# Relu-squared attention into an MLP mixer: a straight last step of the first batch, residual transposes issued per step, channel units ahead of the transposes of x, and another order of weight loads

## Chip, cores and metric

One NeuronCore of a Trainium2 chip. The time is device microseconds (us) of one execution. A lower time is better. A run was compared with runs of the kernel before on the same chip, and only fast runs count for the times: some executions of the same kernel run at a lower granted TensorE clock for a while.

Engines are named as the profile names them: PE is TensorE's matrix multiplication, PEld its weight loads, DVE VectorE, ACT ScalarE, POOL GpSimd, SP SyncE (it issues the DMA transposes here).

## The reference

```python
# q, k, v: (8, 12, 448, 64);  d_model = 12*64 = 768;  token width 256;  channel width 1536
scores = (1/sqrt(64)) * q @ k.T
attn   = relu(scores)**2 / 448
x      = (attn @ v)  as (8, 448, 768)                       # heads side by side
u      = x + (relu(x.T @ w_tok1) @ w_tok2).T                # token mixing
out    = u + relu(u @ w_ch1) @ w_ch2                        # channel mixing
```

## The kernel before

Four heads form a **quad**; there are 24, three (DB) per batch item. **Step i** computes the scores of quad i and, for quad i-1, the values (attention times v), the transposes of x, and token mixing (`token1`, `token2`). When the three quads of a batch item are mixed, its channel mixing is put in a queue of **units**: a `channel1` unit is 6 matmuls, 12 units per batch item; `channel2` units are 12 matmuls. `fill` puts units at set places between the other work, to cover PE's waits. From quad 6 on, the transposes of x are DMA transposes issued by SyncE; before that, PE does them. Steps 0 to 3 have a hand-written order; step 3 is the last of the first batch item, and the first step with units to run.

```python
    def values_out(i):                       # scale quad i's values into xT, on DVE
        ...
        for r in range(2):
            nc.vector.tensor_scalar(out=xT[b % 2][:, 2 * d + r, :S], in0=ps[:, r, :S], ...)

    def x_back(i):                           # x with tokens on partitions
        ...
        if i >= XDMA:                        # XDMA = 6: by DMA
            for r in range(2):
                nc.sync.dma_start_transpose(out=x_sb[:, r], in_=xT[b % 2][:, 2 * d + r, :])
            return
        ...                                  # else 8 PE transposes into ps, then
        nc.vector.tensor_copy(...)           # one copy of 1024 columns to x_sb

    def u_back(b):                           # the residual u, tokens on partitions
        t = chunks(b)
        u_tiles[b] = mix.tile([128, NP, NT - NT // 2, 128], BF16, name="u_sb", bufs=3)
        for p in range(NP):                  # NP = 6
            nc.sync.dma_start_transpose(out=u_tiles[b][:, p, : len(t), :],
                                        in_=uT_tiles[b // 2][:, p, t.start * 128 : t.stop * 128])

    def channel_work(b):                     # after token2 of the batch item's last quad
        u_back(b)
        for e in range(EC):                  # EC = 12
            queue.append((C1, lambda e=e: channel1(b, e)))
        ...                                  # channel2 units too

    for i in range(DB + 1):                  # steps 0 to 3
        for c in range(QC):                  # seven chunks of scores
            if i == DB and c < 2:            # step 3
                square()
                values(i - 1, ((4,), (5, 6))[c])
                if c == 1:
                    values_out(i - 1)
            scores(i, c)
            ...
            if i < DB: ...
            else:                            # step 3
                if c == 0: token2(i - 2, early=True)
                if c == 2: x_back(i - 1)
                if c == 3: token1(i - 1)
                if c == 4: transposes(i + 1); token2(i - 1, early=True); channel_work(0)
                if c == 5: fill(1 / 4)
        if i == 1: load_four(4); load_wc1(1, 2)
        if i == 2: load_four(5); load_wc2(0, 4)
        if i == 3: load_four(6); load_wc2(1, 4)
    square()
    fill(1 / 4)

    for i in range(DB + 1, ND + 2):          # steps 4 and on
        ...                                  # scores 0, 1; values(i - 1); values_out(i - 1); scores 2
        x_back(i - 1)
        ...                                  # loads of quad i + 3
        fill(1 / 3)
        ...                                  # scores 3, 4; transposes of q and k of quad i + 1
        fill(2 / 9)
        token1(i - 1)
        fill(1 / 9, least=1)
        ...                                  # scores 5, 6; token2(i - 1); channel_work
        fill(1 / 3)
```

## Time and profile before

| | kernel before |
|---|---|
| time, median of 3 runs | 386.91 us (386.85 to 387.58) |
| span of the profiled run | 385.1 us |
| PE busy | 363.2 us, 94% |
| last-ending chain: PE / DMA | 82% / 10% |

The page's chain of work that ended last, and one of its costliest groups (line, engine, operation, shapes, count; busy us, mean ns of one; idle time just before, and what ended most of it):

```profile
PE 82%; DMA 10%; POOL 3%; DVE 2%; ACT 1%; issue 1%; ACTq 0%
...
L248 PE MATMUL t_ps<-x_sb,wt 128*128 128x256 bf16 x192 | 24.9, 273 | 3.3 <-DMA x_sb<-xT 2.8
```

PE makes most of the chain, but a tenth of it is transfers. The second line is `token1`: of the 3.3 us for which PE stood idle before it in the whole run, 2.8 were for x_sb, which a DMA transpose brings (2.25 of them at one place, near 131 us). The other waits are shown in the prediction.

### The profile page before, as it was taken

How to read it: one execution, taken by the hardware profiler on the slowest of the kernel's cores; microseconds unless marked ns; L12 is line 12 of the kernel's file. 1: busy time of each engine (PE TensorE's matmuls, PEld its weight loads, DVE VectorE, ACT ScalarE, POOL GpSimd, SP SyncE). 2: the span in 40 equal slices, each digit the busy share in tenths (PEclk: the TensorE clock that was granted, in tenths of full speed). 3: DMA queues.
4: the chain of work that ended last, by engine and by line, in shares of the span. 5: the costliest groups of instructions: out<-in, count | busy, mean ns of one | idle time of the engine just before them, and what ended most of it. 6: DMA issues, size and time to landing. Idle time of an engine off the chain costs nothing.

```text
span 385.1 us, 10018 instructions
## 1 busy us (share of the span) xinstructions
PE 363.2 (94%) x4281; PEld 198.9 (52%) x4281; DVE 207.1 (54%) x375; ACT 212.2 (55%) x295; POOL 99.5 (26%) x178
## 2 busy tenths in 40 slices
PE   6778889999999799999999999999999999999995
PEld 2344445544555455555545655555555555555563
DVE  2898657672585565555654756545744755121022
ACT  4987677676465246764676455764576455411400
POOL 9974254503303123303213213123120000000000
PEclk9999999999999999999999999999999999999999
DMA  8999999995549497598449677498453433334024
GB/s 155 130 193 174 179 184 110 188 152 72 78 102 175 102 167 128 63 138 155 97 72 113 122 144 133 61 128 138 115 74 66 92 78 74 64 63 107 2 52 112
DMA packets 72045, 43.82 MB, mean 114 GB/s; under 512 B 46080, under 2 KB 68544, under 8 KB 72000
## 3 DMA queue, kind: packets, MB, share of 16 engines
q0 software_dynamic: 24448, 21.47, 42.0%
q1 hardware_dynamic: 47248, 21.28, 30.5%
q8 instruction: 33, 0.54, 0.6%
q10 hardware_dynamic: 304, 0.43, 0.4%
q14 instruction: 12, 0.10, 0.1%
HBM read 43.38 MB, written 11.01 MB: 141 GB/s over the span
## 4 chain that ended last, share of the span: by engine, by line
PE 82%; DMA 10%; POOL 3%; DVE 2%; ACT 1%; issue 1%; ACTq 0%
PE m_ps L327 28%; PE m_ps L310 27%; PE sc_ps L163 8%; PE acc_ps L191 7%; PE t_ps L248 5%; PE h_ps L272 4%; DMA wc<-in_moe_w_ch_dram 4%; DMA k_raw<-in_k_dram 3%; PE qkT_ps L142 2%; DMA x_sb<-xT 2%; DMA k_first<-in_k_dram 1%; ACT at L172 1%; POOL q_raw L83 1%; DVE xT L205 1%; POOL k_raw L83 1%
## 5 line engine op out<-in xcount | busy, mean ns | idle before, releaser
L172 ACT ACTIVATE at<-sc_ps 128x896 bf16<-128x896 f32 x168 | 144.7, 922 | 60.5 <-PE sc_ps L163 60.5
L310 PE MATMUL m_ps<-uT_sb,wc 128*128 128x448 bf16 x576 | 117.8, 353 | 0.6 <-DVE uT_sb L280 0.6
L327 PE MATMUL m_ps<-wc,r_sb 128*128 128x384 bf16 x672 | 115.3, 326 | 0.0
L179 DVE TENSOR_TENSOR at<-at 128x896 bf16<-128x896 bf16 x168 | 98.5, 626 | 6.1 <-ACT at L172 5.9
L317 ACT ACTIVATE r_sb<-m_ps 128x448 bf16<-128x448 f32 x96 | 52.2, 544 | 65.7 <-PE m_ps L310 65.1
L327 PEld LDWEIGHTS <-r_sb 128*128 128x128 bf16 x672 | 64.3, 98 | 45.7 <-issue 4.1
L310 PEld LDWEIGHTS <-wc 128*128 128x128 bf16 x576 | 54.4, 98 | 50.0 <-issue 3.8
L334 DVE TENSOR_TENSOR out_sb<-m_ps,u_sb 128x384 f32<-128x384 f32 x56 | 31.1, 555 | 61.1 <-PE m_ps L327 61.1
L163 PE MATMUL sc_ps<-qkT 64*64 64x448 bf16 x672 | 53.3, 368 | 4.3 <-ACT at L172 3.2
L280 DVE TENSOR_TENSOR uT_sb<-h_ps,xT 128x448 bf16<-128x448 f32 x48 | 27.7, 620 | 52.8 <-PE h_ps L272 52.8
L205 DVE TENSOR_SCALAR xT<-acc_ps 128x448 bf16<-128x448 f32 x48 | 27.7, 620 | 29.0 <-PE acc_ps L191 29.0
L473 POOL COPY gate<-x_sb 1x1 bf16<-1x1 bf16 x14 | 3.0, 214 | 146.2 <-DMA x_sb<-xT 146.2
L191 PE MATMUL acc_ps<-at,v_raw 64*64 64x448 bf16 x672 | 38.3, 352 | 0.0
L152 DVE COPY qkT<-qkT_ps 128x896 bf16<-128x896 bf16 x44 | 25.6, 620 | 19.5 <-PE qkT_ps L142 19.5
L83 POOL DMA_DIRECT2D q_raw<-in_q_dram x48 | 28.9, 611 | 25.1 <-DMA wc<-in_moe_w_ch_dram 18.0
L163 PEld LDWEIGHTS <-qkT 64*64 64x64 bf16 x672 | 15.7, 106 | 33.0 <-issue 29.2
L83 POOL DMA_DIRECT2D v_raw<-in_v_dram x48 | 29.4, 636 | 2.4 <-PE qkT_ps L142 1.1
L83 POOL DMA_DIRECT2D k_raw<-in_k_dram x46 | 28.0, 623 | 4.7 <-DMA k_raw<-in_k_dram 2.1
L248 PE MATMUL t_ps<-x_sb,wt 128*128 128x256 bf16 x192 | 24.9, 273 | 3.3 <-DMA x_sb<-xT 2.8
L256 ACT ACTIVATE r_sb<-t_ps 128x512 bf16<-128x512 f32 x24 | 14.3, 598 | 22.8 <-PE t_ps L248 22.8
L191 PEld LDWEIGHTS <-v_raw 64*64 64x64 bf16 x672 | 20.0, 107 | 12.2 <-issue 1.7
L248 PEld LDWEIGHTS <-wt 128*128 128x128 bf16 x192 | 18.5, 98 | 9.7 <-issue 4.0
(30 smaller groups left out, 105.6 us busy)
## 6 DMA issues: line engine op xcount, KB each, us to landing
out_dram<-out_sb SPq DMA_DIRECT2D x54, 192.0 KB, 2.7
q_raw<-in_q_dram POOLq DMA_DIRECT2D x48, 112.0 KB, 4.2
v_raw<-in_v_dram POOLq DMA_DIRECT2D x48, 112.0 KB, 5.2
k_raw<-in_k_dram POOLq DMA_DIRECT2D x46, 112.0 KB, 5.0
wc<-in_moe_w_ch_dram POOLq DMA_DIRECT2D x2, 1152.0 KB, 15.5
wc<-in_moe_w_ch_dram POOLq DMA_DIRECT2D x4, 576.0 KB, 12.5
u_sb<-uT_sb SPq DMA_TRANSPOSE x48, 4.3
x_sb<-xT SPq DMA_TRANSPOSE x36, 2.4
```

What stands on the lines that cost most here:

```text
L83: eng.dma_start(out=dst[64 * r : 64 * (r + 1)].rearrange("p g c d -> p g (c d)"), in_=src[b, h0 : h0 + 2].rearrange("g (p c) d -> p g (c d ...
L163: nc.tensor.matmul(ps[64 * r : 64 * (r + 1), g, :S], lhsT=sb[h, r, 1, c * 64 : (c + 1) * 64], rhs=sb[h, r, 0, :], start=True, stop=True, s ...
L172: nc.scalar.activation(at, ps[:, :, :S], AF.Relu)
L179: nc.vector.tensor_tensor(out=at, in0=at, in1=at, op=ALU.mult)
L191: nc.tensor.matmul(ps[64 * g : 64 * (g + 1), r, :S], lhsT=v_raw[h, g, c, :], rhs=at[h, g, :], start=(c == 0), stop=(c == QC - 1), skip_gro ...
L205: nc.vector.tensor_scalar(out=xT[b % 2][:, 2 * d + r, :S], in0=ps[:, r, :S], scalar1=float(alpha2), scalar2=None, op0=ALU.mult,)
L248: nc.tensor.matmul(ps[:, j, :], lhsT=wt1[:, c, j * 128 : (j + 1) * 128], rhs=x_sb[:, :, c, :], start=(c == 0), stop=(c == 3),)
L280: nc.vector.tensor_tensor(out=uT_tiles[b // 2][:, 2 * d + r, off : off + S], in0=parts[r][:, :S], in1=xT[b % 2][:, 2 * d + r, :S], op=ALU.add,
L310: nc.tensor.matmul(ps[:, :S], lhsT=wc1[:, g, e * 128 : (e + 1) * 128], rhs=uT[:, g, off : off + S], start=(g == 0), stop=(g == CC - 1),)
L317: nc.scalar.activation(r2[:, e, off : off + S], ps[:, :S], AF.Relu)
L327: nc.tensor.matmul(ps[:, :HN], lhsT=r2[:, e, t * 128 : (t + 1) * 128], rhs=wc2[:, e, cols], start=(e == 0), stop=(e == EC - 1),)
L334: nc.vector.tensor_tensor(out=o[:, cols].rearrange("n (g d) -> n g d", d=128), in0=ps[:, :HN].rearrange("n (g d) -> n g d", d=128), in1=u_ ...
```

## The change

Its intent is to close PE's gaps in the first 90 us, and the one near 131 us. It has four parts:

1. **Residual transposes per step.** `token2` issues the two of its own quad at once; no longer do all six go out together at the end of a batch item.
2. **Unit ahead of the transposes of x** in steps 4 to 6.
3. **Load order.** The second half of `w_ch1` goes behind the loads of quad 5, and `w_ch2` goes in two halves, behind step 3 and in step 4, instead of in four quarters from step 2 to step 5.
4. **Step 3 rewritten** straight: all values first; evictions of quad 2 split over DVE and ACT; units 0 and 1 begun in the two banks of the value tile, with the four of six matmuls whose inputs exist; q and k of quad 4 transposed early; units 2 and 3 inside the step (the old step ran two units, the new one runs four).

```diff
@@ token2(i)                                                   (part 1)
+        u_back(i)
-    def u_back(b):
+    def u_back(i):
+        b, d = divmod(i, DB)
         t = chunks(b)
-        u_tiles[b] = mix.tile(...)
-        for p in range(NP):
+        if d == 0:
+            u_tiles[b] = mix.tile(...)
+        for p in (2 * d, 2 * d + 1):
             nc.sync.dma_start_transpose(...)
@@ channel_work(b)
-        u_back(b)
-        for e in range(EC):
+        for e in range(2 if b == 0 else 0, EC):
@@ steps 4 and on                                              (part 2)
+        if i - 1 < XDMA:
+            fill(1 / 3, least=1)
         x_back(i - 1)
         ...
-        fill(1 / 3)
+        if i - 1 >= XDMA:
+            fill(1 / 3)
@@ loads                                                       (part 3)
-        if i == 1: load_four(4); load_wc1(1, 2)
-        if i == 2: load_four(5); load_wc2(0, 4)
-        if i == 3: load_four(6); load_wc2(1, 4)
-        if i in (4, 5): load_wc2(i - 2, 4)
+        if i == 1: load_four(4)
+        if i == 2: load_four(5); load_wc1(1, 2)
+        # after step 3: load_four(6); load_wc2(0, 2)
+        if i == 4: load_wc2(1, 2)
@@ step 3                                                      (part 4)
+    i = DB
+    square()
+    values(i - 1, (4, 5, 6))
+    values_out(i - 1, split=True)          # one half on DVE, one on ACT
+    scores(i, 0)
+    token2(i - 2, early=True)
+    x_back(i - 1, split=True)              # one half on DVE, one on ACT
+    scores(i, 1)
+    token1(i - 1)
+    square(keep=1)
+    first = channel1_begin()               # units 0, 1: matmuls 0 to 3 of each
+    scores(i, 2)
+    token2(i - 1, early=True)
+    square(keep=1)
+    channel1_end(first)                    # matmuls 4, 5 of each; one relu for both
+    scores(i, 3)
+    transposes(i + 1, early=True)
+    square(keep=1)
+    scores(i, 4)
+    channel_work(0)
+    queue.pop(0)[1]()                      # unit 2
+    square(keep=1)
+    scores(i, 5)
+    scores(i, 6)
+    square(keep=1)
+    queue.pop(0)[1]()                      # unit 3
+    square()
```

More of the change, by code (lines that the diff above doesn't have):

```diff
@@ L198, in values, with values_out @@
                     )
-    def values_out(i):
+    def values_out(i, split=False):
         b, d = divmod(i, DB)
@@ L204, in values_out @@
         for r in range(2):
+            if split and r == 1:
+                nc.scalar.activation(
+                    xT[b % 2][:, 2 * d + r, :S], ps[:, r, :S], AF.Copy, scale=float(alpha2)
+                )
+                continue
             nc.vector.tensor_scalar(
@@ L215, with x_back @@
     XDMA = 6
-    def x_back(i):
+    def x_back(i, split=False):
         b, d = divmod(i, DB)
@@ L238, in x_back @@
                 )
+        if split:
+            nc.vector.tensor_copy(x_sb[:, 0].rearrange("n c d -> n (c d)"), ps[:, 0])
+            nc.scalar.copy(x_sb[:, 1].rearrange("n c d -> n (c d)"), ps[:, 1])
+            return
         nc.vector.tensor_copy(
@@ L292, in chunks @@
         return range(half) if b % 2 == 0 else range(half, NT)
-    def u_back(b):
+    def u_back(i):
+        b, d = divmod(i, DB)
         t = chunks(b)
-        u_tiles[b] = mix.tile([128, NP, NT - NT // 2, 128], BF16, name="u_sb", bufs=3)
-        for p in range(NP):
+        if d == 0:
+            u_tiles[b] = mix.tile([128, NP, NT - NT // 2, 128], BF16, name="u_sb", bufs=3)
+        for p in (2 * d, 2 * d + 1):
             nc.sync.dma_start_transpose(
@@ L303, in channel1 @@
     def channel1(b, e):
-        if b % 2 == 0 and e == 0:
+        if b % 2 == 0 and e == 0 and b > 0:
             r2_tiles[b // 2] = mix.tile([128, EC, 2 * S], BF16, name="r2_sb")
@@ L317, in channel1, with channel1_begin, channel1_part, channel1_end @@
         nc.scalar.activation(r2[:, e, off : off + S], ps[:, :S], AF.Relu)
+    def channel1_begin():
+        r2_tiles[0] = mix.tile([128, EC, 2 * S], BF16, name="r2_sb")
+        first = ps_acc.tile([128, 2, 512], FP32, tag="acc", name="m1_ps2")
+        for e in range(2):
+            channel1_part(first, e, range(CC - 2))
+        return first
+    def channel1_part(ps, e, gs):
+        for g in gs:
+            nc.tensor.matmul(
+                ps[:, e, :S],
+                lhsT=wc1[:, g, e * 128 : (e + 1) * 128],
+                rhs=uT_tiles[0][:, g, :S],
+                start=(g == 0),
+                stop=(g == CC - 1),
+            )
+    def channel1_end(ps):
+        for e in range(2):
+            channel1_part(ps, e, range(CC - 2, CC))
+        nc.scalar.activation(r2_tiles[0][:, :2, :S], ps[:, :, :S], AF.Relu)
     def channel2(b, t, half):
@@ L406 @@
     transposes(0, early=True)
-    for i in range(DB + 1):
+    for i in range(DB):
         for c in range(QC):
-            if i == DB and c < 2:
-                square()
-                values(i - 1, ((4,), (5, 6))[c])
-                if c == 1:
-                    values_out(i - 1)
             scores(i, c)
             square(keep=1)
-            if c < 3 and 0 < i < DB:
+            if c < 3 and i > 0:
                 values(i - 1, (4 + c,))
@@ L419 @@
                     values_out(i - 1)
-            if i < DB:
-                if c == 3:
-                    transposes(i + 1, early=True)
-                if c == 4 and i > 0:
-                    x_back(i - 1)
-                if c == 5:
-                    values(i, (0, 1))
-                if c == 6:
-                    if i > 0:
-                        token1(i - 1)
-                    values(i, (2, 3))
-                if c == 0 and i > 1:
-                    token2(i - 2, early=True)
-            else:
-                if c == 0:
-                    token2(i - 2, early=True)
-                if c == 2:
-                    x_back(i - 1)
-                if c == 3:
-                    token1(i - 1)
-                if c == 4:
-                    transposes(i + 1)
-                    token2(i - 1, early=True)
-                    channel_work(0)
-                if c == 5:
-                    fill(1 / 4)
+            if c == 0 and i > 1:
+                token2(i - 2, early=True)
+            if c == 3:
+                transposes(i + 1, early=True)
+            if c == 4 and i > 0:
+                x_back(i - 1)
+            if c == 5:
+                values(i, (0, 1))
+            if c == 6:
+                if i > 0:
+                    token1(i - 1)
+                values(i, (2, 3))
         if i == 1:
             load_four(4)
-            load_wc1(1, 2)
         if i == 2:
             load_four(5)
-            load_wc2(0, 4)
-        if i == 3:
-            load_four(6)
-            load_wc2(1, 4)
+            load_wc1(1, 2)
+    i = DB
     square()
-    fill(1 / 4)
+    values(i - 1, (4, 5, 6))
+    values_out(i - 1, split=True)
+    scores(i, 0)
+    token2(i - 2, early=True)
+    x_back(i - 1, split=True)
[8 more added lines that the diff above has]
+    scores(i, 3)
+    transposes(i + 1, early=True)
+    square(keep=1)
[8 more added lines that the diff above has]
+    square()
+    load_four(6)
+    load_wc2(0, 2)
+    rate[0] = len(queue) * C1 / DB
     for i in range(DB + 1, ND + 2):
@@ L474 @@
             load_four(i + PRE)
-        if i in (4, 5):
-            load_wc2(i - 2, 4)
+        if i == 4:
+            load_wc2(1, 2)
         square()
-        fill(1 / 3)
+        if i - 1 >= XDMA:
+            fill(1 / 3)
         if i < ND:
```

## The prediction

> **What bounds the kernel now.** I read the page first, then the busy time by stretches, TensorE's order of time, who waited for whom, and SyncE's order of time. The page says that TensorE (PE) is the bound, with little idle time left in all:
>
> ```profile
> PE 363.2 (94%) x4281; PEld 198.9 (52%) x4281; DVE 207.1 (54%) x375; ACT 212.2 (55%) x295; POOL 99.5 (26%) x178
> PE   6778889999999799999999999999999999999995
> DMA  8999999995549497598449677498453433334024
> ```
>
> Idle PE time is 385.1 - 363.2 = 21.9 us. The second line puts nearly all of it in the first nine of 40 slices (to 87 us), in one slice near 130 us and in the last slice. The third says that the transfers are as full as can be for just those nine slices. The stretches give sizes (columns: stretch, its length, busy PE, PEld, DVE, ACT, POOL, granted clock, DMA share, GB/s):
>
> ```profile
> 30.00:40.00 10.00, 7.74 (x133) 4.23 (x132) 8.46 (x16) 7.21 (x10) 4.33 (x7) 1.00 1.26 177
> 40.00:50.00 10.00, 8.26 (x137) 4.20 (x136) 5.88 (x11) 6.74 (x10) 2.73 (x5) 1.00 1.28 179
> 70.00:80.00 10.00, 9.50 (x145) 5.11 (x144) 7.13 (x13) 7.38 (x11) 3.58 (x6) 1.00 1.30 172
> 120.00:140.00 20.00, 17.75 (x209) 10.03 (x211) 12.01 (x23) 7.47 (x10) 3.74 (x7) 1.00 0.82 146
> 140.00:160.00 20.00, 20.00 (x291) 10.95 (x284) 11.40 (x21) 13.16 (x19) 3.84 (x8) 1.00 0.59 107
> ```
>
> Before 30 us the program is not changed, and after 140 us PE has no idle time until the end. So what can be won lies in 30 to 90 us (2.3 + 1.7 + 0.7 + 1.2 + 0.5 + 0.6 = 7.0 us) and in the one gap of 2.25 us near 131 us: **9.2 us, 2.4%, is the ceiling**. PE's order of time names the waits (start, duration, what, and in brackets the idle time before it):
>
> ```profile
> 34.55 0.93 PE L230 MATMUL x_ps<-ident,xT 128*128 128x128 bf16 x8 [1.06 <-DVE xT L205]
> 36.26 1.03 PE L248 MATMUL t_ps<-x_sb,wt 128*128 128x256 bf16 x8 [0.47 <-DVE x_sb L239]
> 39.89 1.29 PE L310 MATMUL m_ps<-uT_sb,wc 128*128 128x448 bf16 x6 [0.60 <-DVE uT_sb L280]
> 45.30 0.93 PE L230 MATMUL x_ps<-ident,xT 128*128 128x128 bf16 x8 [0.55 <-DVE xT L205]
> 49.18 0.41 PE L142 MATMUL qkT_ps<-ident,k_raw 64*64 64x64 bf16 x26 [1.06 <-DMA k_raw<-in_k_dram]
> 87.09 1.03 PE L248 MATMUL t_ps<-x_sb,wt 128*128 128x256 bf16 x8 [0.56 <-DMA x_sb<-xT]
> ```
>
> The first three are the step that the change rewrites (head quads counted from 0: the scores of quad 3, the mixing of quad 2). The fourth recurs at 57.90 (0.55) and 69.05 (0.54). Two further waits, 0.43 us each, are for ACT's relu at 66.44 and 77.59.
>
> The gap near 131 us is read from SyncE, whose queue goes in order:
>
> ```profile
> 119.33 1.11 SPq L346 DMA_DIRECT2D out_dram<-out_sb  x2
> 120.48 7.91 SPq L298 DMA_TRANSPOSE u_sb<-uT_sb  x6
> 128.49 3.42 SPq L223 DMA_TRANSPOSE x_sb<-xT  x2
> ...
> 133.33 1.03 PE L248 MATMUL t_ps<-x_sb,wt 128*128 128x256 bf16 x8 [2.25 <-DMA x_sb<-xT]
> ```
>
> Six residual transposes of a finished batch hold the queue for 7.91 us. The transpose that token mixing needs had its input at 125.1 us and went out only at 128.49.
>
> **What the Trainium skill says.** (1) "DMA: Bandwidth & Descriptors", Queues, rings and completion order: each DMA engine takes turns between the queues that have work, packet by packet. The trace agrees in effect: the two transposes issued at 24.59 and 25.91, beside a full load queue, landed 9.2 and 9.8 us later, while at 96.56 and 97.95, with the queue nearly empty, two took 2.4 and 2.5. (2) The same page, Issuing engines are not separate DMA queues: all transfers end on the same 16 engines, whoever issues them. Agrees: the share stays above 1 from 20 to 86 us. (3) "ScalarE: Activation LUTs", What ACT_TABLE_LOAD costs: an ACTIVATE with immediate scale costs 186 ns + 0.833 ns per column. That is 559 ns for 448 columns; this trace has 544 for its 448-column relu, and DVE takes 620 for the same size. So halving the evictions onto both engines saves about one 0.53 us pass. On which PSUM bank a tile gets, and so whom it waits for, I rely on the order of instructions with its waits, not on a page.
>
> **The change, part by part.** The order of instructions shows the same number of PE rows (8564), so no work is removed; from quad 7 on, PE's order is identical. Only waits can change.
>
> *Step 3.* All values of quad 2 come first, and then the mixing chain runs between scores. I laid it out by hand from 30.8 us with measured durations (four value matmuls 0.19, four score matmuls 0.25, token stages 0.87, a channel unit 1.14, a relu of 896 columns 0.81 back to back, an eviction 0.54 to 0.62). Values end at 32.0, as the last square is ready at 31.75. The split eviction is done at 32.7, but the transposes must wait until the first h bank is added on DVE (33.3): idle 0.5. The split x_sb copy is done at 34.75: idle 0.4. Token1 ends at 35.6; the eight partial channel matmuls (8 x 0.19 = 1.5 us) fill the wait for its relu; token2 ends at 38.2; the last four channel matmuls wait for the two adds to 39.0: idle 0.7. Then ACT becomes the limit: the double relu (0.92), a relu of scores, and its half of the early q/k eviction follow each other, and PE waits 0.4 for the bank of unit 2, 0.7 for the last scores, 0.4 for the next step's. Values of quad 3 begin at about 45.3 with four channel units done. Before they began at 43.08 with two done: 43.08 + 2 x 1.14 = 45.36. **Step 3: about 0, +-0.8.**
>
> *Steps 4 to 6.* A unit now stands ahead of the transposes of x, so 0.55 + 0.55 + 0.54 = **1.65 us** go. The loads of quad 5 go ahead of the second half of the first weight, so the 1.06 us wait for k goes: in the old order k landed at 49.1, behind that half (44.1); by moving ahead of its 7 us it lands at about 43. The half itself then lands near 51.8 (the same bytes, in the other order), and unit 6, its first user, comes at about 51.8: at most a few tenths. One more step ends without a unit, as the steps 5 and 6 do: -0.4. **Sum to the values of quad 6: 1.65 + 1.06 - 0.4 = 2.3 us**, at 75.6 instead of 77.95.
>
> *Given back at token1 of quad 6.* Its x_sb comes by DMA. In the kernel before, the loads issued by GpSimd keep their queue full without a break from 20 us until 85.3 us (last landing of quad 9), and the four transposes behind them landed at 85.3, 85.9, 86.3 and 87.0. The change moves no bytes out of this backlog. With everything 2.3 us earlier, PE wants x_sb at 84.2, and it comes at about 85.4 (between 84.5 by the share that the transposes had at the end of the backlog, and 87.0 if they again wait for its end). So **of 2.3 us about 1.5 remain** (0 to 2.3).
>
> *The gap at 131 us.* Two residual transposes per step (2 x 1.25 us) fit between the adds of token2 (issue at about 121.3, done at 123.9) and the values' eviction (125.1). Then x_sb goes out at 125.1 to 127.6 and lands 2.5 us later, at about 130.1, before PE asks at 131.1. **2.25 us go.** For the first two batches splitting changes nothing: SyncE has nothing else queued and already transposes each pair as it is added (24.59, 32.93, 39.87).
>
> Sum: 1.5 + 2.25 = 3.7 us, 386.9 - 3.7 = **383.2 us**.
>
> **Rivals.** *A: the front is won in full.* If x_sb gets its turn among the loads at once, and ACT keeps up in step 3 (+0.8), it is 386.9 - (2.3 + 0.8 + 0.6 + 2.25) = 381.0. Against: the 7 to 12 us that each transpose issued from 24 to 79 us took to land. *B: the load backlog decides alone.* Then token1 of quad 6 stays at 87.0, all the front's gain is lost, and only the gap at 131 us counts: 386.9 - 2.3 = 384.6. The stretches show 45 GB/s instead of some 190 from 58 to 62 us; if that falls worse, the same. *C: a new wait.* The weight's second half is late for unit 6, or the pair of transposes now delays x_sb in every later step, some tenths in each of 13: 386 to 388. Against: 1 to 1.2 us of slack by the above, and x_sb lands well before its use in all later steps of the trace.
>
> **Range and chances.** A and B bound the likely: 381.0 to 384.6; half a us is added at the upper side for C and for a step 3 slower than I laid out. 80%: 381.2 to 385.4. Over 2% faster needs 379.2, 7.7 of the 9.2 us that are idle at all: 0.02. Over 2% slower: 0.01.
>
> **What would show it.** Right: no wait of PE over 0.3 us near 130 us; no waits for xT at the transposes of quads 3 to 5, none for k of quad 5; PE waits for ACT in step 3's second half; a wait for x_sb of 1 us or more before token1 of quad 6, which begins at 85 to 86.5; the last load of quad 9 lands at 84 to 87. Wrong: token1 of quad 6 before 84 (A), after 87 (B), or waits over 0.5 us that are new after 90 us (C).

## The result, and the profile after

The changed kernel took **383.88 us median** (382.72 to 384.18, four runs) against 386.88 (386.27 to 387.58) for the kernel before, measured beside it. The ratio is **0.9916, 95% interval 0.989 to 0.9943**: within 2%, and inside the predicted range. A ratio is the mean time of one kernel's fast runs over the mean of the other's fast runs of the same rounds, so it is not quite the ratio of the medians.

The page of the kernel after, with the lines that answer to those shown of before:

```profile
PE 365.0 (95%) x4281; PEld 200.8 (53%) x4281; DVE 205.5 (54%) x373; ACT 214.4 (56%) x297; POOL 98.1 (26%) x176
PE   6787899999999999999999999999999999999995
...
PE 87%; ACT 4%; DMA 3%; DVE 2%; POOL 2%; issue 1%; ACTq 0%
...
L257 PE MATMUL t_ps<-x_sb,wt 128*128 128x256 bf16 x192 | 25.5, 277 | 0.8 <-ACT x_sb L246 0.8
```

The 7 in the 14th slice (near 130 us) is gone, transfers make 3% of the chain where they made 10%, and `token1` no longer waits for DMA. SyncE's order of time shows how the gap near 130 us closed (start, duration, what):

```profile
119.05 1.11 SPq L380 DMA_DIRECT2D out_dram<-out_sb  x2
120.48 2.51 SPq L310 DMA_TRANSPOSE u_sb<-uT_sb  x2
124.31 2.50 SPq L228 DMA_TRANSPOSE x_sb<-xT  x2
```

Two residual transposes take 2.51 us where six took 7.91, so the transposes that `token1` needs go out at 124.31 instead of 128.49. PE's order of time at the places where the kernel before waited (a wait would stand in brackets):

```profile
51.60 0.61 PE L235 MATMUL x_ps<-ident,xT 128*128 128x128 bf16 x8
...
86.81 1.04 PE L257 MATMUL t_ps<-x_sb,wt 128*128 128x256 bf16 x8
...
130.64 1.04 PE L257 MATMUL t_ps<-x_sb,wt 128*128 128x256 bf16 x8
```

No brackets: neither the transposes of quad 3, nor `token1` of quad 6, nor that of quad 9 waits. The x_ps group also takes 0.61 us instead of 0.93, which comes up again below.

**A trap in comparing the two traces.** `token1` of quad 6 starts at 86.81 us, hardly before the 87.09 of the kernel before, because the profiled run of after lost time at its start, where PE's program is the same (of the loads, only those behind quad 4's differ, issued from 27 us on): the values ahead of step 3 begin at 33.55 instead of 30.80 us. The trace of after has three spells of half granted clock there (from 8.94, 19.18 and 29.42 us, 3.41 us each). A second trace of the kernel *before* has them too (9.31, 19.55, 29.79), and has these values at 33.65. They come with the run. So I measure from step 3 on, between marks: A is the first of the value matmuls of quad 2 that run into step 3 (the first eight, 0.40 us, still belong to step 2, in every version), then the values of quad 3, the values of quad 6, `token1` of quad 6, `token1` of quad 9, and the end. All in us, from PE's order of time:

| run (first name = what it is; see below) | A at | A to values 3 (step 3) | values 3 to 6 | to token1 of 6 | to token1 of 9 | to the end |
|---|---|---|---|---|---|---|
| before, first trace | 30.80 | 12.27 | 34.88 | 9.14 | 46.24 | 251.75 |
| e0, before again | 33.65 | 12.28 | 33.65 | 8.41 | 46.52 | 253.32 |
| **after** | 33.55 | 15.26 | 29.58 | 8.41 | 43.83 | 251.75 |
| **e14, after again** | 31.39 | 15.51 | 29.58 | 8.41 | 43.92 | 251.78 |
| e1, part 1 alone | 32.32 | 12.28 | 33.65 | 8.41 | 43.83 | 251.83 |
| e4, part 2 alone | 32.42 | 12.27 | 30.88 | 8.41 | 46.15 | 253.43 |
| e3, part 3 alone | 32.09 | 12.27 | 33.63 | 8.41 | 47.13 | 251.73 |
| e6, part 4 alone | 31.97 | 15.52 | 32.33 | 8.41 | 46.50 | 251.63 |
| e2, after without part 1 | 31.64 | 15.52 | 29.59 | 8.41 | 46.06 | 253.44 |
| e7, parts 1 to 3 | 32.28 | 12.28 | 30.89 | 8.41 | 43.83 | 251.80 |
| e10, e7 with units moved | 32.11 | 12.27 | 29.03 | 8.39 | 43.83 | 251.77 |
| e12, after with units moved | 31.17 | 15.22 | 31.98 | 8.41 | 43.83 | 251.68 |

From A to the end this is 354.3 us before (354.2 in e0) and 348.8 after (349.2 in e14). In e12 a half-clock spell from 45.13 to 48.55 us lies across the second and the third column. In the columns 12.28 and 15.51 are not alike: the new step 3 runs four units and the old one two, and a unit's pitch, from one to the next with PE busy, is 1.14 us.

### The profile page after: what moved, and what is told of

It is laid out like the page before. It is cut to its first block, busy times and chain, and to the rows that moved or that the text cites. A ratio compares the mean times of both kernels' runs of the same rounds, so it can differ in the third digit from the quotient of the medians.

```text
span 382.4 us, 10027 instructions
## 1 busy us (share of the span) xinstructions
PE 365.0 (95%) x4281; PEld 200.8 (53%) x4281; DVE 205.5 (54%) x373; ACT 214.4 (56%) x297; POOL 98.1 (26%) x176
## 4 chain that ended last, share of the span: by engine, by line
PE 87%; ACT 4%; DMA 3%; DVE 2%; POOL 2%; issue 1%; ACTq 0%
PE m_ps L361 29%; PE m_ps L322 28%; PE sc_ps L163 9%; PE acc_ps L191 8%; PE t_ps L257 5%; PE h_ps L281 4%; PE qkT_ps L142 3%; ACT at L172 2%; DMA wt_nat<-in_moe_w_tok_dram 2%; DMA k_first<-in_k_dram 1%; PE x_ps L235 1%; DVE uT_sb L289 1%; DVE at L179 1%; PE m_ps L340 1%; POOL wt L106 1%
## 5 line engine op out<-in xcount | busy, mean ns | idle before, releaser
L322 PE MATMUL m_ps<-uT_sb,wc 128*128 128x448 bf16 x564 | 115.3, 353 | 0.6 <-DVE qkT L152 0.6
L361 PEld LDWEIGHTS <-r_sb 128*128 128x128 bf16 x672 | 64.3, 98 | 45.7 <-issue 3.9
L329 ACT ACTIVATE r_sb<-m_ps 128x448 bf16<-128x448 f32 x94 | 51.2, 544 | 58.8 <-PE m_ps L322 58.4
L322 PEld LDWEIGHTS <-wc 128*128 128x128 bf16 x564 | 53.2, 98 | 50.1 <-issue 4.9
L163 PE MATMUL sc_ps<-qkT 64*64 64x448 bf16 x672 | 54.4, 370 | 5.6 <-ACT at L172 4.2
L281 PE MATMUL h_ps<-wt,r_sb 128*128 128x448 bf16 x96 | 22.5, 355 | 0.6 <-POOL wt L106 0.6
```

What stands on the lines that cost most here:

```text
L163: nc.tensor.matmul(ps[64 * r : 64 * (r + 1), g, :S], lhsT=sb[h, r, 1, c * 64 : (c + 1) * 64], rhs=sb[h, r, 0, :], start=True, stop=True, s ...
L281: nc.tensor.matmul(parts[r][:, :S], lhsT=r1[:, j, r * 128 : (r + 1) * 128], rhs=wt2[:, j, :], start=(j == 0), stop=(j == JC - 1),)
L322: nc.tensor.matmul(ps[:, :S], lhsT=wc1[:, g, e * 128 : (e + 1) * 128], rhs=uT[:, g, off : off + S], start=(g == 0), stop=(g == CC - 1),)
L329: nc.scalar.activation(r2[:, e, off : off + S], ps[:, :S], AF.Relu)
L361: nc.tensor.matmul(ps[:, :HN], lhsT=r2[:, e, t * 128 : (t + 1) * 128], rhs=wc2[:, e, cols], start=(e == 0), stop=(e == EC - 1),)
```

## The experiments

Three calls of four kernels; the kernel before ran beside each call (medians 387.24, 388.13, 387.8 us over 11 runs each, single runs from 384.36 to 389.92). All results were correct.

### Which part carries the gain?

The theory after the result: part 1 carries most, part 2 something, part 3 is doubtful, and part 4 costs as much as it brings. The rival: the new step 3 is the gain, and the rest is small.

**e0: the kernel before, unchanged**, to learn what two runs of the same kernel differ by.

> The kernel before, unchanged, profiled a second time. It tells what of the difference between the two profiles is none of the change. The changed kernel's profile has three spells of half clock before 33 us (granted clock 0.985 over the span) and its step 3 begins at 33.55 us instead of 30.80 although the program up to there is the same. If such spells come with the run or the chip, this profile may have them too, and its step 3 will begin at 32 to 34 us; if only the changed kernel had them, clock 1.0 and 30.8 us again. Also: are the last loads of quad 9 again landed at 85.3 us, with the fall to 45 GB/s from 58 to 62 us, or nearer 81.6 as in the changed kernel. Time: ratio 1.000 within 0.003.

388.38 us (387.34 to 389.63), ratio 1.0017 (0.9963 to 1.0071). So 0.4 to 0.7% either way is noise in three rounds. Its trace was worth more than its time: the wait of 1.06 us for k of quad 5, which the prediction counted on, is **not in it**, as PE's order of time shows (in the first trace this group stands split, with the wait ahead of its last 26 transposes):

```profile
50.77 0.43 PE L142 MATMUL qkT_ps<-ident,k_raw 64*64 64x64 bf16 x28
```

**e1: part 1 alone**, on the kernel before.

```diff
@@ token2
+        u_back(i)
@@ channel_work
-        u_back(b)
@@ u_back: two transposes per call, as in the change
```

> The kernel before with the residual transposes issued per step, nothing else. Theory (the queue of SyncE held x_sb up): the 2.25 us wait near 131 us goes and nothing else changes, 386.9 - 2.25 = 384.6 us, ratio 0.994. Rival (the wait is contention of the transfers, not the order of the queue, or pairs of transposes bring new waits): 386 to 387, with a wait for x_sb somewhere after 90 us.

383.89 us (383.15 to 385.32), ratio **0.9918** (0.9878 to 0.9957): about as much as the whole change. It is 3.2 us at 387.2, more than the 2.25 us of the wait. The reason stands in the stretches just after the wait (stretch, its length, busy PE, PEld, DVE, ACT, POOL, granted clock, DMA share, GB/s). First the wait, from PE's order of time of e0, the kernel before again; then the stretches of e0, and of e1:

```profile
134.51 1.03 PE L248 MATMUL t_ps<-x_sb,wt 128*128 128x256 bf16 x8 [2.53 <-DMA x_sb<-xT]
```

```profile
136.00:140.00 4.00, 4.00 (x21) 1.56 (x19) 0.56 (x1) 0.69 (x2) 2.51 (x5) 0.62 1.10 188
```

```profile
136.00:140.00 4.00, 4.00 (x54) 2.14 (x52) 2.90 (x7) 2.62 (x3) 0.00 (x0) 1.00 0.72 92
```

Both show PE busy for all of the 4 us, but e0 got 21 matmuls done in it and e1 54. They are not the same matmuls, so the counts alone prove nothing; the granted clock does. It is 0.62 in e0 there: the gap was followed by 3.41 us at half clock (from 135.6 us). Six of the profiles have the gap (2.05 to 3.14 us long); in **three** (e0, e2, e4) such a spell begins within 1.1 us of its end, in three (before, e3, e6) it doesn't. The last column of the table gives its price: 253.3 to 253.4 us with it, 251.6 to 251.8 without, so 1.6 us. None of the seven profiles of fast runs without the gap has a spell there. The wait thus costs 2.25 us every time and 1.6 us more about every second time: 2.25 + 0.8 = 3.05, against 3.2 timed.

**e2: the changed kernel without part 1** (six transposes per batch item again; the diff of e1 the other way).

> The changed kernel with the six residual transposes of a batch issued together again. Theory: the wait of about 2.25 us for x_sb near 128 to 131 us comes back, 383.9 + 2.25 = 386.1 us; then the front of the change brings only about 0.8 us. Rival (front gains were the larger part): 384.5 or less.

386.12 us (384.4 to 387.95), ratio 0.9968 (0.9926 to 1.0011). The gap is back (2.05 us) with its half-clock spell (from 131.26 us). Without part 1 the rest of the change is not shown to be faster than the kernel before.

**e7: parts 1 to 3, with the old step 3.**

```diff
+ part 1, part 2 and part 3 as in the change
  for i in range(DB + 1):   # steps 0 to 3 as in the kernel before
```

> The kernel before with split residual transposes, the new order of loads and a unit ahead of the transposes of x, but with the old step 3. Theory (step 3 is worth about nothing, front parts 2.7 us of which some is given back at x_sb of quad 6): 383 to 384 us, within 1 us of the changed kernel. Rival (step 3 carries the gain): 385 or more. Rival (step 3 costs): below 383.

**381.04 us** (379.31 to 382.01), ratio **0.983** (0.9789 to 0.987): leaving out the rewritten step 3 makes the kernel no slower, and faster than the first comparison had the change (0.989 to 0.9943). The second comparison of the change, e14 below, has 0.9827 to 0.9879, which overlaps with e7, so the times alone do not settle the size. The table does, as no half-clock spell lies between its marks here: A to `token1` of quad 6 takes 12.28 + 30.89 + 8.41 = 51.58 us in e7, 53.25 in after, 53.50 in e14 and 53.52 in e2. **The rewritten step costs 1.7 to 1.9 us**, and the rival theory falls.

### Parts 2, 3 and 4 alone

**e4: part 2 alone.**

```diff
+        if i - 1 < XDMA:
+            fill(1 / 3, least=1)
         x_back(i - 1)
...
-        fill(1 / 3)
+        if i - 1 >= XDMA:
+            fill(1 / 3)
```

> The kernel before, with only the unit of channel work put ahead of the transposes of x in steps 4 to 6. Prediction on record: three waits of 0.55 us go, 1.65 us. From the second profiles of before and of the variant without the new step 3, where the way from the values of quad 3 to those of quad 6 took 33.65 and 30.89 us: 2.8 us, 0.92 per step, for the second half of the transposes waits for the second eviction too (0.53 us later). So 33.65 to about 30.9 us on that way, and ratio about 0.993; if the 2.8 us came from the loads instead, 33.6 stays.

384.42 us, one of its runs (391.61) slow; ratio 0.9894 (0.9849 to 0.9939). The way from values 3 to 6 shrinks from 33.65 to 30.88, so by **2.77 us**, not by the 1.65 of the three waits that the profile names. The missing part was inside the group of transposes: the eight have two inputs, evicted one after the other on DVE, and the wait in brackets is only that for the first. PE stood again for the second, and the group's length hid it: 0.93 us with the wait, 0.61 without (both lines are shown above, here and in the prediction). 0.55 + 0.32 = 0.87 per step, 2.6 for three; the last 0.17 us is not accounted for.

**e3: part 3 alone.**

```diff
-        if i == 1: load_four(4); load_wc1(1, 2)
+        if i == 1: load_four(4)
-        if i == 2: load_four(5); load_wc2(0, 4)
+        if i == 2: load_four(5); load_wc1(1, 2)
-        if i == 3: load_four(6); load_wc2(1, 4)
+        if i == 3: load_four(6); load_wc2(0, 2)
-        if i in (4, 5): load_wc2(i - 2, 4)
+        if i == 4: load_wc2(1, 2)
```

> The kernel before, with only the new order of loads. Prediction on record: 1.06 us (the wait for k of quad 5). The second profile of before had no such wait (k landed at 47.1, wanted at 50), so the theory now is: nothing, ratio 1.000, no wait for k in either profile; k of quad 5 lands at about 39. Rival: the order of loads carries part of the gain, way from quad 3 to quad 6 below 33.

387.4 us, ratio 0.9993 (0.9946 to 1.004); values 3 to 6 takes 33.63 as in e0. k of quad 5 does land earlier (40.6 us), but in the old order it landed at 45.7 to 47.1 in e0, e1, e4 and e6, before PE wanted it. The 49.1 of the first trace was an accident of that run. **Part 3 is worth nothing in these traces.** Whether it spares a run that would have had the accident was not tested.

**e6: part 4 alone**, the new step 3 with the old loads, the old residual transposes and the units behind the transposes of x.

```diff
@@ the changed kernel
- parts 1, 2 and 3
+ as in the kernel before; fill(1 / 3, least=1) behind x_back for steps 4 to 6
```

> The kernel before with only the new step 3 (split evictions, two units begun in value banks, early q/k transposes, units 2 and 3 inside); residual transposes per batch, old loads, units behind the transposes of x. Prediction on record: 0 +-0.8 us. After eight runs the theory is that it costs: step 3 from 12.3 to 15.4 us with two more units (2.28 us), so +0.8, and +0.9 in step 4, whose unit behind token2 had been nearly free: 1.7 us slower, ratio 1.004, with the wait near 131 us as before. Rival: the cost is an interplay with the unit-first order; then ratio 1.000 or below.

388.17 us (386.26 to 389.34), ratio 0.9997 (0.997 to 1.0025). The trace has the loss: A to `token1` of quad 6 takes 15.52 + 32.33 + 8.41 = 56.26 us against 54.34 in e0, 1.9 more, as between e7 and after. The times do not show it: 1.9 us would be 1.005, outside the interval. The kernel before itself has waits in some runs that it lacks in others (its first trace took 56.29 us for the same way), so part of the loss may be hidden by that. Part may be the clock: over the 33 runs of the kernel before, a mean granted clock lower by 0.01 goes with about 2 us more, and e6's runs had 0.991 where the kernel before beside them had 0.988, so by estimate 0.5 us in e6's favour. The rest of the contradiction stays open. The traces of e7 and of the changed kernel are the firmer evidence.

### Where does the new step 3 lose?

Two theories. *ACT:* the step gives ACT more work and delays it, and the four units then have to share its end with the relus of the scores. *Place of the units:* units 2 and 3 were taken from places in step 4 where they cost little.

PE's order of time in the new step 3 of the changed kernel, then ACT's, then DVE's:

```profile
37.82 1.03 PE L257 MATMUL t_ps<-x_sb,wt 128*128 128x256 bf16 x8 [0.82 <-ACT x_sb L246]
...
41.88 0.35 PE L340 MATMUL m_ps<-uT_sb,wc 128*128 128x448 bf16 x1 [0.34 <-DVE uT_sb L289]
...
44.70 1.30 PE L322 MATMUL m_ps<-uT_sb,wc 128*128 128x448 bf16 x6 [0.57 <-DVE qkT L152]
```

```profile
35.40 0.54 ACT L206 ACTIVATE xT<-acc_ps 128x448 bf16<-128x448 f32 x1 [1.15 <-DVE xT L210]
...
37.18 0.58 ACT L246 COPY x_sb<-x_ps 128x512 bf16<-128x512 bf16 x1 [0.43 <-DVE x_sb L245]
...
43.17 0.92 ACT L351 ACTIVATE r_sb<-m_ps 128x896 bf16<-128x896 f32 x1 [1.53 <-PE m_ps L340]
```

```profile
34.74 0.62 DVE L210 TENSOR_SCALAR xT<-acc_ps 128x448 bf16<-128x448 f32 x1 [0.69 <-PE acc_ps L191]
...
36.73 0.42 DVE L245 COPY x_sb<-x_ps 128x512 bf16<-128x512 bf16 x1 [0.17 <-PE x_ps L235]
```

**The two halves of each split eviction do not run beside each other.** DVE's half of xT ends at 34.74 + 0.62 = 35.36, and ACT, idle for 1.15 us, begins its half at 35.40. DVE's half of the copy ends at 37.15, and ACT begins at 37.18. It is so in all six profiles with the split (after, e14, e2, e6, e12, e13). So the split copy takes 0.42 + 0.03 + 0.58 = 1.03 us where the whole one took 0.69 on DVE alone, and `token1` waits 0.82 instead of 0.47; the split values take 1.20 where two passes on DVE took 1.15. For the copy the Trainium skill gives a reason, "PSUM — Partial Sum Buffer", PSUM bank collisions raise a hardware error: two engines must not be on the same bank at once, reads included, so a program has to put them one after the other; and the x_ps tile, 1024 columns of two bytes, is one bank of 2 KiB. The trace agrees, with 0.03 us between the halves. The values lie in two banks of one tile, so that rule does not ask for an order there, yet it is there. It is not the common destination: the q and k copies of quad 1, from two PSUM tiles into one destination tile, start at 11.26 on DVE and 11.30 on ACT and do overlap. What else orders the halves of the values is open.

So ACT, idle early, gets its work late: in this step it has taken over 0.54 + 0.58 us of evictions and 0.91 us of the early q and k copy, and from 43.17 us to the end of the step it is busy without a break, with relus and that copy, while PE waits. The step took 15.51 us where 12.28 + 2 x 1.14 = 14.56 would be the old step with two more units: **0.95 lost** (0.70 in the first trace of after).

**e12: the changed kernel with units 2 and 3 moved out of step 3** into steps 4 to 6, as in e7.

```diff
     channel_work(0)
-    queue.pop(0)[1]()
     square(keep=1)
     scores(i, 5)
     scores(i, 6)
-    square(keep=1)
-    queue.pop(0)[1]()
     square()
@@ steps 4 to 6: one unit at each of these places
+    PLAN = {4: 'ABCD', 5: 'ABC', 6: 'ABC'}   # A ahead of x_back, B ahead of token1, C behind token1, D behind token2
```

> The changed kernel with units 2 and 3 taken out of step 3 and put into steps 4 to 6 where the variant without the new step 3 has them. It asks why the new step 3 costs 1.7 us. Theory A (ACT is starved early in the new step and sets its end): without the two units step 3 shortens only by their relus, 15.5 to about 14.7 us against 12.3 of the old order, and the whole is 0.3 to 0.8 us slower than the changed kernel. Theory B (the order is as good, but the two units were taken from holes where they were nearly free): step 3 shortens by 2.3 us to about 13.2, and the whole is about 1.4 us faster than the changed kernel.

384.98 us (384.1 to 387.62), ratio 0.9931 (0.989 to 0.9972): not faster than after. Step 3 took 15.22 us with two units less, against 15.26 and 15.51; the last 1.3 us of it lie in the half-clock spell, which by estimate (half of that time) cost it some 0.6. Taking away 2 x 1.14 us of units thus shortened it by less than 1 us. The rest turned into waits for ACT, in PE's order of time, ahead of the spell:

```profile
42.82 0.38 PE L163 MATMUL sc_ps<-qkT 64*64 64x448 bf16 x4 [0.83 <-ACT at L172]
...
44.44 0.38 PE L163 MATMUL sc_ps<-qkT 64*64 64x448 bf16 x4 [1.24 <-ACT at L172]
```

So in the new step ACT sets the end, and the units inside it cost less than half of their pitch. The second theory looks at where they came from. In step 4 a unit stood behind `token2`. e7, which has it, and after, which has not, both from `token2` to the next values:

```profile
52.59 0.93 PE L272 MATMUL h_ps<-wt,r_sb 128*128 128x448 bf16 x4
53.36 1.30 PE L313 MATMUL m_ps<-uT_sb,wc 128*128 128x448 bf16 x6
...
54.99 1.49 PE L191 MATMUL acc_ps<-at,v_raw 64*64 64x448 bf16 x28
```

```profile
56.88 0.93 PE L281 MATMUL h_ps<-wt,r_sb 128*128 128x448 bf16 x4
...
58.69 0.38 PE L163 MATMUL sc_ps<-qkT 64*64 64x448 bf16 x4 [0.43 <-ACT at L172]
59.05 1.52 PE L191 MATMUL acc_ps<-at,v_raw 64*64 64x448 bf16 x28
```

2.40 us with a unit, 2.17 without: the unit costs **0.23** there and not 1.14, as PE waits for ACT's last relus anyway. Taking it away saves 0.23, and the trace agrees: values 3 to 6 is 29.58 + 2 x 1.14 = 31.86 with after's eight units made up to ten, against 30.89 in e7: 0.97 lost, where 1.14 - 0.23 = 0.91 is expected.

0.95 and 0.97 add up to the 1.7 to 1.9 us, but both charge a unit inside step 3 with its full pitch, which e12 shows it does not cost there. So they are a way of counting and not two causes. e12 has e7's ten units at e7's places and only the step itself new, and its step 3 takes about 14.6 us (15.22 less the 0.6) against 12.28 in e7: **the new order of the step alone loses about 2.3 us.** Units 2 and 3 then cost 0.65 to 0.9 us inside it, and would cost 1.31 outside (30.89 in e7 less 29.58), so their place gives 0.4 to 0.65 back. That is what the first theory (ACT) had expected of e12, step 3 at about 14.7 us and the whole 0.3 to 0.8 us slower than the changed kernel; the second had expected 13.2 us and 1.4 us gained. Which of the things handed to ACT weighs most was tested for the split alone (e13, below).

### Is there a better version?

If a unit behind `token2` costs 0.23 and elsewhere 1.14, the units in steps 5 and 6 stand in the wrong place too.

**e10: e7 with the unit of steps 5 and 6 that stood ahead of token1 moved behind token2.**

```diff
+    PLAN = {4: 'ABCD', 5: 'ACD', 6: 'ACD'}   # e7 had one ahead of token1 (B) and none behind token2 (D) in 5, 6
```

> Old step 3, split residual transposes, new loads, unit first, and in steps 5 and 6 the unit between the q/k transposes and token1 moved behind token2. Theory: a unit behind token2 falls into PE's wait for ACT (from token2 to the values 2.40 us with a unit, 2.17 without), so it costs 0.23 us there and 1.14 where it stood: 2 x 0.91 = 1.8 us less than the variant without this move (381.0): 379.2 us, no wait of 0.43 us for ACT any more. Rival (ACT sets the pace of the steps anyway): no change.

**380.08 us** (379.21 to 380.31), ratio **0.9793** (0.9758 to 0.9829), with e11 below the best: beside the same runs of the kernel before it gains 8 us. The interval overlaps that of e7; the trace shows the step between them. They were run at other times. Values 3 to 6 went from 30.89 to 29.03, so 1.86 us for two moved units; 2 x 0.91 = 1.82 was to be expected.

**e11: e10 with two value chunks of quads 1 and 2 ahead of the early transposes of x.**

```diff
-                if c == 4 and i > 0:
-                    x_back(i - 1)
-                if c == 5:
+                if c == 4:
                     values(i, (0, 1))
+                    if i > 0:
+                        x_back(i - 1)
```

> The variant with units in holes, and in steps 1 and 2 two chunks of values ahead of the transposes of x instead of behind one scores group later. PE waits there for the DVE half of the early q/k eviction (1.60 us in step 2, 0.8 to 1.6 in step 1); eight value matmuls take 0.38 us. Theory: 0.4 us less in each, 0.8 us in all: way from token1 of quad 1 unchanged, start of step 3 earlier by 0.8. Rival: the squares these values need come later on DVE than the eviction, no gain or a loss.

379.73 us; ratio 0.9803 (0.9761 to 0.9845), not distinguishable from e10. One of its six runs, the profiled one, counts as slow (385.22), and another is nearly as long but counts as fast (384.24); the other four took 379.2 to 379.8. The slow one shows a danger that the prediction feared for the changed kernel, first in PE's order of time and then in the stretches:

```profile
85.53 1.86 PE L248 MATMUL t_ps<-x_sb,wt 128*128 128x256 bf16 x8 [4.35 <-DMA x_sb<-xT]
```

```profile
84.00:88.00 4.00, 2.47 (x11) 1.52 (x12) 0.00 (x0) 0.51 (x1) 2.50 (x5) 0.50 0.27 32
```

The transposes of x for quad 6 went out at 74.86 and 76.18 us, the loads ended at 85.05, the transposes landed at 85.39, PE waited 4.35 us and then had half clock. In the other profiles the loads end at 78.9 to 81.8 and nobody waits, but for the first trace of the kernel before (85.34, and a wait of 0.56). I did not find out what makes a run's loads slower.

**e13: e11 with the old step 3's two evictions of quad 2 split over DVE and ACT**, as in the change.

```diff
-                    values_out(i - 1)
+                    values_out(i - 1, split=True)
...
-                    x_back(i - 1)
+                    x_back(i - 1, split=True)
```

> The variant before in this call, with the old step 3 but its two evictions for x (values, and x_sb) halved between DVE and ACT as the changed kernel does. Theory: the halves are the useful part of the new step 3, the transposes' second half and token1 start 0.4 to 0.5 us sooner each: step 3 from 12.28 to about 11.4 us. Rival: ACT, which has relus of scores waiting, loses what DVE wins: no change.

381.61 us (379.54 to 385.19), ratio 0.9839 (0.98 to 0.9877): no gain, and an interval that overlaps e11's. In PE's order of time `token1` of quad 2 waits longer, not shorter, than the 0.47 us of the kernel before:

```profile
37.22 1.20 PE L257 MATMUL t_ps<-x_sb,wt 128*128 128x256 bf16 x8 [1.23 <-ACT x_sb L246]
```

DVE's half of the copy runs from 36.13 to 36.55 us and ACT's from 36.59 to 37.17, one after the other here too. But most of the wait comes ahead of the copy: PE has made its transposes at 35.21, and DVE's half stands behind a square that waited for ACT, which had taken over the other half of the values. In DVE's order of time:

```profile
35.59 0.63 DVE L179 TENSOR_TENSOR at<-at 128x896 bf16<-128x896 bf16 x1 [1.42 <-ACT at L172]
36.13 0.42 DVE L245 COPY x_sb<-x_ps 128x512 bf16<-128x512 bf16 x1
```

So the split brings nothing in the old step either; in the trace it costs. (A half-clock spell from 37.96 us follows, so the 14.31 us that step 3 takes from A in this trace overstate the loss.)

**e14: the changed kernel again, unchanged**, beside e11 and e13.

> The changed kernel again, beside the variants of this call: ratio to before 0.991 to 0.993; step 3 15.3 to 15.5 us; no wait near 131 us and no spell of half clock after 50 us.

382.51 us (381.57 to 383.4), ratio 0.9853 (0.9827 to 0.9879). This is better than the 0.991 to 0.993 that was expected, and the interval does not touch that of the first comparison, 0.989 to 0.9943. So the size of the gain is known to about 3 to 5.7 us, not better. e14 is still slower than e11 beside it, by 2.8 us in the medians.

## Why the prediction was right, and where its steps were not

The total was right: 3.7 us predicted; 3.0 and 5.7 measured in two comparisons, and 5.0 to 5.5 between the traces from A to the end (where one trace of the kernel before has the accident at k and the other a half-clock spell). **Its steps were right only for part 1, and for part 2 in kind; that the rest of the sum came out is luck, as its errors cancel.**

- **The gap at 131 us ("2.25 us go"): right, and undersized.** The mechanism and the times hold: the transposes issued at 124.31 us (predicted 125.1), no wait at 130.64 (131.1). The term lacked the half-clock spell that the gap brings on in three of six profiles, 1.6 us each (e0, e2, e4).
- **Unit ahead of the transposes of x ("1.65 us go"): right, mis-sized.** Measured 2.77 (e4). The bracket counts the idle time before a group, not the standstill within it.
- **The wait for k of quad 5 ("1.06 us goes"): wrong.** It was in one execution only. I took one trace's wait for a property of the kernel, though the same trace had a stretch of 45 GB/s where about 190 was usual, which I had seen and quoted under rival B. Measured 0 (e3).
- **"One more step ends without a unit: -0.4": right, mis-sized.** Measured 0.97 (e7 against after).
- **Step 3 "about 0, +-0.8": wrong on what the split does; the size is at the edge of what I allowed.** Measured 0.70 to 0.95 us lost, apart from the 0.97 above. The step that failed is "halving the evictions onto both engines saves about one 0.53 us pass": the halves run one after the other, which saves nothing on the values and costs 0.34 on the copy (a wait of 0.82 for ACT instead of the 0.4 that I laid out). ACT as the limit of the step's second half came as laid out, and e12 confirms it; by e12 the order of the step costs 2.3 us with the units elsewhere.
- **"0.8 given back at x_sb of quad 6": wrong for the changed kernel's runs.** The last load of quad 9 landed at 81.56 us, not at 84 to 87; x_sb landed at 84.85, ahead of PE's 86.81. So the sign that was named for it, a wait of 1 us or more before `token1` of quad 6, did not show. The 85.3 us belong to the first trace, with its slow stretch; in e0 the last load landed at 81.1. The effect exists in some runs: 0.56 us in the first trace of before, 4.35 in the slow run of e11.

"Before 30 us the program is not changed" holds for PE, but not for the loads, which part 3 changes from 27 us on; nothing here hangs on it.

As a sum against e0, the kernel before without the accident: part 2 gives +2.77, part 3 0, part 4 takes 1.7 to 1.9, so the front gives 0.8 to 1.1 (predicted 1.5); the gap gives 2.25 and about half of 1.6. That is 3.9 to 4.1 us.

Of the rivals, A was half right: x_sb did get its turn in time. But the full front was not won, as step 3 lost what A had it gain. B's backlog did not decide. C did not come: no wait over 0.5 us is new after 90 us.

## What to carry to other kernels

Price a gap of the bound engine with what may follow it (here 1.6 us of half clock after three of six gaps of 2 to 3 us), and see a wait in a second trace of the same kernel before counting on its removal: 1.06 of the 2.3 us predicted for the front were one run's accident. Put filler work where the bound engine waits for another anyway (0.23 us a unit) and not where it would run (1.14). An eviction split over two engines gains only if its halves really overlap and the second engine has nothing queued that others wait for, so look at both engines' start times before you give the next bound more work.

## What the Trainium skill lacked or had wrong

- "TensorE: Matmul & The Clock Gate", Part 1: The HAM clock gate, has the PE clock fall to half after an idle window of some 3.4 us, the windows free-running, at a cost of half the throttled time. The length and the cost agree: spells of 3.41 us that begin whole multiples of that apart (9.31, 19.55, 29.79 and 135.6 us in e0), 1.6 us lost in each behind the gap. What is lacking is a single gap shorter than the window, which can do it too. Gaps of 2.05, 2.16 and 2.53 us were followed by a spell, gaps of 2.25, 2.50 and 3.14 us were not, so the length alone does not decide. Counting windows of 3.41 us back from each run's own spells, PE was busy for 0.32 (e0), 0.37 (e4) and 0.40 (e2) of the window that held most of the gap where a spell followed, and for 0.42 in each of the three where none did; six cases are not a rule.
- "DMA: Bandwidth & Descriptors", DMA Transpose (X-bar), gives no time that one transpose of this size holds SyncE's queue: two took 2.51 us of it and six 7.91, so 1.26 and 1.32 us each, and whatever is issued behind them waits for that. Nor does the page tell how long such a small transfer takes beside a full queue: 9.2 to 9.8 us here, against 2.4 to 2.5 with a nearly empty one (the first trace of before).
- No page that I read tells of the order between two engines that evict two different banks of one PSUM tile: ACT began 0.03 to 0.04 us after DVE's end in all six profiles.
